# Moving five of the six transpose turns of the mixed features of batches 3 and 4 one slot later

## Chip, cores, metric

The kernel runs on one core of a Trainium2 chip. The metric is the device time of one execution in microseconds (us). All runs told of here are of the fast state (none is over 1.5% above the fastest of its kernel); TensorE's granted clock is 0.992 to 1.0 of full speed on average over an execution. That last per cent matters below.

## The reference, in short

```python
# 1. mLSTM cell over q, k, v and gates: (4 batches, 8 heads, 768 tokens, 40) -> x (4, 768, 320)
# 2. Fourier mix and MLP on x:
mixed = np.real(np.fft.fft(np.fft.fft(x, axis=1), axis=2))
u = x + mixed
un = (u - mean(u)) / np.sqrt(var(u) + 1e-06)          # over the 320 features
out = u + np.maximum(un @ w_ch1, 0.0) @ w_ch2         # 320 -> 1280 -> 320
```

## The kernel before

The four batches are pipelined. Work is put down in slots, and each engine's program is the list of its instructions sorted by slot and phase. While the second layer of the MLP of batch n-1 runs on TensorE (`po`, one block of 20 products in most slots), batch n's features are mixed in. For each of six token chunks, in the order c = 0, 5, 1, 4, 2, 3, this is

- an addition on VectorE of the mixed features `pu` (in PSUM) to x, and the statistics of the sum (lines 746 to 757 of the profile);
- a turn: centring on ScalarE (`uc`, L765), three transposes on TensorE (`put`, L772), a copy from PSUM on ScalarE (`uT`, L777).

Two chunks share one `pu`: 0 and 5, 1 and 4, 2 and 3. For batches 3 and 4 (b = 2 and 3 in the code) the PSUM banks are pinned:

```python
# cut from several places; NT = 6 chunks, TG = 3; DM = 320, HALF_D = 160, NC = 161
ORDER = (0, 5, 1, 4, 2, 3)
...
MIX = {"z": (2, 3), "zt": 2, "u": (3, 2, 2), "ut": (3, 3, 3, 3, 2, 3)}
# pu of chunks 0/5: bank 3; of 1/4 and of 2/3: bank 2.
# put in ORDER: bank 3, but bank 2 for c=2
...
def mix_add(b, c):
    k = mixes[b]
    k.u = xs[b]
    ops = (OP.subtract, OP.add) if c >= NT // 2 else (OP.add, OP.subtract)
    u, n = k.u[:, c, 0:DM], HALF_D - 1
    pu = k.pu[min(c, NT - 1 - c)]
    P, Q = pu[:, 0:NC], pu[:, NC:DM]
    if c == TG:
        own = pu[0:1, DM + 1:]
        if b == 0:
            nc.vector.tensor_copy(out=pu[0:1, 0:HALF_D], in_=own[:, 0:HALF_D])
            nc.vector.tensor_copy(out=pu[0:1, HALF_D:DM + 1], in_=backwards(own, HALF_D, NC))
        else:
            nc.vector.tensor_copy(out=P[0:1], in_=own)
            nc.vector.memset(Q[0:1], 0.0)
    if b == 0:
        nc.vector.tensor_tensor(out=u, in0=u, in1=pu[:, 0:DM] if c < TG else backwards(pu, DM, DM), op=OP.add)
    else:
        nc.vector.tensor_tensor(out=u[:, 0:NC], in0=u[:, 0:NC], in1=P, op=OP.add)
        nc.vector.tensor_tensor(out=u[:, NC:], in0=u[:, NC:], in1=backwards(P, n, n), op=OP.add)
        nc.vector.tensor_tensor(out=u[:, 1:HALF_D], in0=u[:, 1:HALF_D], in1=Q, op=ops[0])
        nc.vector.tensor_tensor(out=u[:, NC:], in0=u[:, NC:], in1=backwards(Q, n - 1, n), op=ops[1])
    stats = st_p.tile([L, 6], FP, name="stats", tag="stats")
    nc.vector.bn_stats(stats, u[:, 0:DM])
    nc.vector.bn_aggr(k.u[:, c, DM:], stats)

def mix_center(b, c):
    k = mixes[b]
    u = k.u[:, c]
    uc = k.uc[c] = st_p.tile([L, 2, L + 64], FP, name="uc", tag="uc")
    twice = bass.AP(tensor=u.tensor, offset=u.offset, ap=[list(u.ap[0]), [L, 2], [1, L + 64]])
    nc.scalar.activation(out=uc, in_=twice, func=AF.Identity, scale=-1.0, bias=u[:, DM:DM + 1])

def mix_turn(b, c):
    k = mixes[b]
    pt = k.pt[c] = bank("put", [L, 3, L], MIX["ut"][ORDER.index(c)] if b > 1 else None)
    for ch in range(3):
        nc.tensor.transpose(pt[:, ch, :], k.uc[c].rearrange("p two n -> p (two n)")[:, ch * L:(ch + 1) * L], ident)

def mix_turn_out(b, c):
    k = mixes[b]
    n = ORDER.index(c)
    nc.scalar.copy(out=uT_bufs[n // TG][:, :, n % TG, :], in_=k.pt[c])
```

The plan of additions (a), and of the three parts of a turn (t). The phases in a slot are EVAC = 0, FILL = 1, MAIN = 2, FILL_PE = 3; the `po` block and its two residuals (L949 on VectorE, x = x + rstd * po) are at MAIN, so an addition at MAIN + 0.5 stands behind both residuals of its slot.

```python
    for c, a, t in zip(ORDER, s_add, s_turn):
        at(a, FILL if b < 2 else MAIN + 0.5, mix_add, b, c)
        at(t, FILL + 0.1, mix_center, b, c)
        at(t, FILL_PE + (5 if b == 0 or c in ORDER[:4] else -0.1), mix_turn, b, c)
        if b > 0:
            at(t, FILL_PE + 6, mix_turn_out, b, c)
        elif t < s_mlp:
            at(t + 1, FILL + 0.2, mix_turn_out, b, c)
        else:
            at(t + 1, EVAC, mix_turn_out, b, c)
...
# in plan_batch, batches 2 to 4
        feat = [s_mix + c for c in ((3, 4, 6) if b == 1 else (3, 4, 7))]
        add = [s_mix + c for c in ((4, 4, 5, 6, 7, 7) if b == 1 else (4, 4, 5, 6, 8, 9))]
        turn = [s_mix + c for c in ((5, 6, 6) if b == 1 else (5, 6, 7))]
        late = [s_mix + c for c in ((7, 8, 8) if b == 1 else (8, 9, 10))]
```

The last slot of a batch's stage is s_mix + 11; then the next stage, the first MLP layer (`pm`), begins with sums of `uT` on VectorE (L885).

## Time and profile before

| | before |
|---|---|
| median time | 427.93 us (4 executions) |
| span of the profiled execution | 425.2 us |
| TensorE busy | 409.2 us, 96% |
| TensorE waiting for the last addition, ahead of `put` | 4.3 us in 2 waits |
| batch 3's stretch: first `pu` of batch 3 to first `pm` of batch 3 | 238.06 to 277.20: 39.14 us |
| batch 4's stretch: from there to the `pm` of batch 4 that waits for L885 | 277.20 to 360.50: 83.30 us |

The two stretches hold everything that the change touches; I measure by them below. How the wait of batch 3 is read is shown in the prediction. Its twin in batch 4, on TensorE's timeline of the kernel before (start, duration, what, idle time before it and what ended it):

```profile
349.02 1.52 PE L999 MATMUL po<-T,S 128*128 128x160 f32 x10
350.38 1.52 PE L999 MATMUL po<-w_sb,S 128*128 128x160 f32 x10
354.04 0.52 PE L772 MATMUL put<-ident,uc 128*128 128x128 f32 x3 [2.13 <-DVE x L754]
```

Groups of ten `po` products start 1.36 apart; the prediction reckons from this how late `put` came (step a).

### The profile page before, as it was taken

The page shows a single profiled execution, that of the slowest core. Times are in us where ns is not written, and L with a number is a line of the kernel's source. Part 1 is how long each engine was busy: PE and PEld are TensorE (multiplying, and loading weights), DVE is VectorE, ACT ScalarE, POOL GpSimd, SP SyncE. Part 2 cuts the span into 40 slices and gives each one's busy share as a digit, 9 for nine tenths or more (in the row PEclk, how much of TensorE's full clock was granted, in tenths as well). Part 3 has the DMA queues.
Part 4 walks back from the last instruction along what each step waited for, and adds up shares of the span by engine and source line. Part 5 has one row for each costly group of instructions (what it writes and reads, how often), then busy time and mean ns, then how long its engine had stood idle before and what let it go on. Part 6 is the DMA issues. An engine that isn't in the chain of part 4 may idle for free.

```text
span 425.2 us, 7994 instructions
## 1 busy us (share of the span) xinstructions
PE 409.2 (96%) x2966; PEld 302.7 (71%) x2966; DVE 288.4 (68%) x682; ACT 189.8 (45%) x493; POOL 113.1 (27%) x194
## 2 busy tenths in 40 slices
PE   8999999999999999999999999799999997999997
PEld 6877555566567777776459998776459996445996
DVE  7789895767986557878655768778554785334552
ACT  6986376586651233554563343454450122355000
POOL 5654201468332421250401431440300000020000
DMA  7889297657664244267000725200000000000010
GB/s 227 271 240 341 70 280 239 195 192 216 220 175 144 79 129 145 89 198 217 2 0 2 216 82 179 77 15 1 0 2 0 32 32 32 0 2 0 15 47 32
DMA packets 20549, 47.14 MB, mean 111 GB/s; under 512 B 2784, under 2 KB 9312, under 8 KB 20384
## 3 DMA queue, kind: packets, MB, share of 16 engines
q1 hardware_dynamic: 20512, 46.65, 35.5%
q8 instruction: 23, 0.38, 0.4%
q14 instruction: 14, 0.11, 0.1%
HBM read 42.52 MB, written 4.11 MB: 110 GB/s over the span
## 4 chain that ended last, share of the span: by engine, by line
PE 86%; DVE 9%; ACT 3%; issue 1%; POOL 0%; ACTq 0%; DVEq 0%
PE po L999 18%; PE pm L897 17%; PE po L943 8%; PE ps L465 6%; PE ph L486 5%; PE pm L837 5%; PE pm L902 5%; PE ph L479 4%; PE pu L729 4%; PE px L535 2%; PE put L772 2%; DVE S L985 2%; PE pz L698 2%; PE pm L841 1%; PE pc L496 1%
## 5 line engine op out<-in xcount | busy, mean ns | idle before, releaser
L949 DVE SCALAR_TENSOR_TENSOR x<-po,rstd,x 128x160 f32<-128x160 f32 (+1 forms) x69 | 27.1, 395 | 44.5 <-PE po L999 37.9
L906 DVE TENSOR_TENSOR h<-h,pm 128x384 f32<-128x384 f32 x60 | 30.5, 550 | 33.1 <-ACT h L919 24.7
L443 POOL TENSOR_SCALAR_AFFINE_SELECT W<-W 128x1024 f32<-128x1024 f32 x18 | 21.4, 1190 | 91.0 <-ACT W L421 70.6
L421 ACT ACTIVATE W<-W,colT 128x128 f32<-128x128 f32 x144 | 45.1, 395 | 0.0
L943 PE MATMUL po<-w_sb,h 128*128 128x320 f32 x120 | 34.4, 435 | 0.0
L471 DVE TENSOR_TENSOR W<-ps,W 128x512 f32<-128x512 f32 x48 | 30.7, 680 | 4.5 <-POOL W L443 4.3
L897 PE MATMUL pm<-uT,w_sb 128*128 128x384 f32 x90 | 32.8, 492 | 0.2 <-DVE uT L885 0.2
L777 ACT COPY uT<-put 128x384 f32<-128x384 f32 x24 | 11.3, 478 | 48.5 <-PE put L772 48.5
L837 PE MATMUL pm<-uT,w_sb 128*128 128x384 f32 x80 | 29.7, 500 | 0.7 <-DVE x L749 0.5
L943 PEld LDWEIGHTS po<-w_sb,h 128*128 128x128 f32 x120 | 22.2, 190 | 9.5 <-issue 0.8
L999 PE MATMUL po<-T,S 128*128 128x160 f32 x180 | 27.8, 301 | 0.5 <-DVE x L949 0.4
L465 PE MATMUL ps<-qk 40*128 40x128 f32 x384 | 27.8, 284 | 0.0
L792 POOL TENSOR_TENSOR t<-rstd 128x6 f32<-128x6 f32 x12 | 2.9, 244 | 91.9 <-DVE v L790 91.3
L999 PE MATMUL po<-w_sb,h 128*128 128x160 f32 x180 | 26.2, 301 | 1.1 <-DVE h L906 1.1
L999 PEld LDWEIGHTS po<-T,S 128*128 128x128 f32 x180 | 25.5, 190 | 2.2 <-DVE x L949 1.4
L999 PEld LDWEIGHTS po<-w_sb,h 128*128 128x128 f32 x180 | 24.9, 190 | 2.8 <-DVE h L906 2.4
L465 PEld LDWEIGHTS ps<-qk 40*128 40x128 f32 x384 | 23.4, 187 | 4.2 <-issue 0.7
L486 PE MATMUL ph<-W,kvt 128*41 128x128 f32 x384 | 25.8, 276 | 0.0
L431 POOL TENSOR_TENSOR qg<-qk,Gb 128x512 f32<-128x512 f32 x18 | 25.0, 1388 | 0.1
L479 PEld LDWEIGHTS ph<-qg,C 128*128 128x128 f32 x160 | 20.0, 191 | 6.2 <-issue 2.0
L897 PEld LDWEIGHTS pm<-uT,w_sb 128*128 128x128 f32 x90 | 16.2, 190 | 10.9 <-DVE h L906 1.5
L936 ACT ACTIVATE h<-h 128x384 f32<-128x384 f32 x45 | 23.0, 524 | 1.5 <-DVE h L906 1.5
(207 smaller groups left out, 852.8 us busy)
## 6 DMA issues: line engine op xcount, KB each, us to landing
W<-M_d SPq DMA_DIRECT2D x18, 512.0 KB
kvt<-in_kv SPq DMA_DIRECT2D x24, 324.0 KB
qk<-in_qkT SPq DMA_DIRECT2D x48, 160.0 KB
raw<-in_w SPq DMA_DIRECT2D x10, 640.0 KB
Gb<-G_d SPq DMA_DIRECT2D x36, 128.0 KB
so<-in_o SPq DMA_DIRECT2D x24, 160.0 KB
out<-x SPq DMA_DIRECT2D x24, 160.0 KB
ds_sb<-in_dft_s SPq DMA_DIRECT2D x1, 1155.0 KB
```

The lines of the kernel that those rows point to most:

```text
L421: nc.scalar.activation(out=k.W[:, h, :], in_=M, func=AF.Exp, scale=-1.0, bias=colT[:, c, 0, b * H + h:b * H + h + 1])
L431: nc.gpsimd.tensor_tensor(out=k.qg, in0=k.qk[:, 0], in1=k.Gb, op=OP.mult)
L465: nc.tensor.matmul(k.ps[hip][:, p, :], k.qk[r, 1, p, :], k.qk[r, 0, p, :], start=True, stop=True)
L471: nc.vector.tensor_tensor(out=Wv, in0=k.ps[hip], in1=Wv, op=OP.mult)
L479: nc.tensor.matmul(k.ph[:, p, :], k.C[:, p, :], k.qg[:, p, :], start=(p == 0), stop=False, skip_group_check=True)
L486: nc.tensor.matmul(k.ph[hip * 64:hip * 64 + D1, p, :], k.v1[:, 2 * p + hip, :], k.W[:, 2 * p + hip, :], start=(c == 0 and p == 0), stop=Tr ...
L837: nc.tensor.matmul(k.pm[i], w1_sb[:, ch, f0:f0 + L], u[2 * ch], start=(ch == 0), stop=False)
L897: nc.tensor.matmul(bank, w, u, start=start, stop=True, skip_group_check=True)
L906: nc.vector.tensor_tensor(out=h, in0=h, in1=bank, op=OP.add)
L943: nc.tensor.matmul(k.po, hidden(gr, f)[:, i * L:(i + 1) * L], w2_sb[:, f, :], start=(f == 0), stop=(f == NFF - 1))
L949: nc.vector.scalar_tensor_tensor(out=u, in0=po, scalar=k.rstd[:, c:c + 1], in1=u, op0=OP.mult, op1=OP.add)
L999: nc.tensor.matmul(po, a[:, f], w[:, f], start=start and f == 0, stop=f == half - 1, skip_group_check=True)
```

## The change

The intent is to take c=2's transposes away from the place where they wait for the last additions to leave bank 2. The first five turns of batches 3 and 4 go one slot later; the sixth stays, and shares its slot with the fifth.

```diff
-            turn = [s_mix + c for c in ((5, 6, 6) if b == 1 else (5, 6, 7))]
-            late = [s_mix + c for c in ((7, 8, 8) if b == 1 else (8, 9, 10))]
+            turn = [s_mix + c for c in ((5, 6, 6) if b == 1 else (6, 7, 8))]
+            late = [s_mix + c for c in ((7, 8, 8) if b == 1 else (9, 10, 10))]
```

## The prediction

> **What bounds the kernel now.** I read the page's busy shares and chain first, then the list of what TensorE waited for, then the timelines of TensorE, VectorE (DVE) and ScalarE (ACT) in the two stretches that the change touches. Times are us from the span's start.
>
> ```profile
> PE 409.2 (96%) x2966; PEld 302.7 (71%) x2966; DVE 288.4 (68%) x682; ACT 189.8 (45%) x493; POOL 113.1 (27%) x194
> PE 86%; DVE 9%; ACT 3%; issue 1%; POOL 0%; ACTq 0%; DVEq 0%
> PE put L772 <- DVE x L754: 4.3, 2, 2.1
> PE put L772 <- ACT uc L765: 1.3, 4, 0.4
> ```
>
> TensorE is busy 96% and carries 86% of the chain that ended last, so time returns only if TensorE stands still less. Its longest named wait is the third line: the turn's transposes (put, L772) waited twice, 2.1 us each, for the last of VectorE's additions to x (L754). The two waits are one in each of batches 3 and 4. Batch 3's, first TensorE, then VectorE, then ScalarE:
>
> ```profile
> 263.22 0.55 PE L772 MATMUL put<-ident,uc 128*128 128x128 f32 x3
> 263.61 1.52 PE L999 MATMUL po<-T,S 128*128 128x160 f32 x10
> 264.97 1.52 PE L999 MATMUL po<-w_sb,S 128*128 128x160 f32 x10
> 268.62 0.52 PE L772 MATMUL put<-ident,uc 128*128 128x128 f32 x3 [2.13 <-DVE x L754]
> 268.97 1.52 PE L999 MATMUL po<-T,S 128*128 128x160 f32 x10
> ```
> ```profile
> 266.53 0.38 DVE L949 SCALAR_TENSOR_TENSOR x<-po,rstd,x 128x160 f32<-128x160 f32 x1 [0.97 <-PE po L999]
> 266.83 0.31 DVE L746 COPY pu<-pu 1x161 f32<-1x161 f32 x1
> 267.23 0.19 DVE L747 MEMSET pu<- 1x159 f32 x1
> 268.16 0.31 DVE L754 TENSOR_TENSOR x<-x,pu 128x159 f32<-128x159 f32 x1
> 268.51 0.49 DVE L756 BATCH_NORM_STATS2 stats<-x 128x6 f32<-128x320 f32 x1
> 269.04 0.18 DVE L757 BATCH_NORM_AGGREGATE x<-stats 128x2 f32<-128x6 f32 x1
> ```
> ```profile
> 263.81 0.48 ACT L777 COPY uT<-put 128x384 f32<-128x384 f32 x1 [4.33 <-PE put L772]
> 264.18 1.28 ACT L421 ACTIVATE W<-W,colT 128x128 f32<-128x128 f32 x4
> 266.25 0.61 ACT L765 ACTIVATE uc<-x 128x384 f32<-128x384 f32 x1
> ```
>
> The reader is to see a closed loop. The stalled transposes are those of the fifth chunk (c=2); they write PSUM bank 2. The additions of the sixth chunk (c=3) still read that bank, because both chunks share one feature tile, pu. Those additions stand in VectorE's program behind the residual of the very po block that TensorE has just finished (266.53). So TensorE must finish po, then wait for the residual, the two fixes of pu's first row and four additions, before it may overwrite bank 2. Batch 4 has the same figure: po ends, residual at 351.94, last addition at 353.58, transposes at 354.04 after 2.13 us idle.
>
> **What the Trainium skill says.** "PSUM — Partial Sum Buffer", section "PSUM bank collisions raise a hardware error", asks that PSUM be guarded by semaphores by bank and quadrant, not by address. The trace agrees: put starts at 268.62, 0.15 us after the last read of the bank ended (268.16 + 0.31 = 268.47). The same page, "Engine vs sequencer instructions", says that the ScalarE and VectorE queues are strict FIFO; so here: the c=2 centring (uc, 266.25) came after the exponentials that stand ahead of it, though its data had been there since 263.57 (L757 at 263.39, 0.18 long). "Perfetto Trace Analysis", section "Matmuls", wants independent groups to rotate through banks so that evacuation overlaps the next group; bank 2, held by pu and wanted by put, is the place where this kernel doesn't. The page states no cost for such a wait; I take it from the trace.
>
> **The change part by part.** Nothing is added or removed: the engines run the same instructions. A turn is a centring (ACT, 0.61 us), three transposes (PE) and a copy out (ACT, 0.48 us). In batches 3 and 4 the turns of the chunks, in their order c = 0, 5, 1, 4, 2, 3, go one slot later, except the last, which stays; the last two then share a slot. A slot holds one po block of 20 products (10 in every fourth). The instruction orders of the two kernels confirm it: PE now has each put one po block later and, at the end, six put transposes in a row; ACT has the two centrings in a row and then the two copies; POOL and SP are unchanged, and VectorE differs only in buffer numbers.
>
> I count from start to start on TensorE, since its modelled ends overlap. A block of 20 po products takes 2.72 (263.61 to 264.97, twice), an unstalled put 0.33 behind po.
>
> (a) Removed: the c=2 wait. Without it put would start at 263.61 + 2.72 = 266.33; it started at 268.62. That is 2.29 us. Batch 4: 349.02 + 2.72 = 351.74 against 354.04, 2.30 us. Moved behind the next po block, these transposes need bank 2 at about 0.33 (the put now in that place) + 2.72 = 3.05 after 266.33, while VectorE lets it go at 2.29. The wait is covered whole. Sum: -4.6 us.
>
> (b) Removed in batch 3: the wait of the second turn (c=5) for its centring. The po block before it starts at 249.42, so put was due at 252.14 and came at 252.73: 0.59 us. ACT had there a copy, four exponentials, h, so, then uc. In the new order the exponentials run earlier, straight after the four before them, and the place of this put is taken by c=0's, whose centring has only h and so ahead of it. Sum: -0.6 us.
>
> (c) Added in batch 3: the same ACT sequence (copy, four exponentials, h, so, uc) stands before the put that now takes c=2's old place, that of c=4. Today that uc ends at 266.25 + 0.61 = 266.86 and with some 0.05 for the signal put could start at 266.91, against 266.33: 0.58 us that the longer bank wait hides today and that now shows. Sum: +0.6 us, which cancels (b).
>
> (d) Added: the last turn (c=3) comes earlier relative to the additions it needs, since c=2's put no longer stalls in front. Counted from the due time of the put before (266.33, or 351.74): the statistics end at 2.89 (269.04 + 0.18, batch 3) or 2.89 (batch 4, 354.45 + 0.18). ACT starts 0.10 later, works 0.62, and 0.05 for the signal makes 3.66. TensorE reaches this put at 0.33 + 2.72 + 0.33 = 3.38 in batch 4: it waits 0.28 us. In batch 3 it comes there 0.6 later because of (c): no wait. Sum: +0.3 us.
>
> (e) What follows. In batch 4 the next block's entry is gated by VectorE: the residual of the last po block (359.00), then the sums of uT (L885), then pm at 360.50. That tail starts from the end of po, 1.36 us behind the last put; the two copies need about 0.5 after that put, so the tail moves with it. In batch 3 VectorE's mask product (L471, 1.26 us) and residual follow the c=3 additions; they end near 4.3 on the same count, TensorE needs them at about 4.7 (put, put, px): no new wait. Sum: 0.
>
> Total: -4.6 - 0.6 + 0.6 + 0.3 = -4.3 us, so 428.0 becomes 423.7, about 1.0% faster.
>
> **The rivals.**
> First, the wait is only handed on: six transposes at the end of the stage wait for the last centring. For it: ACT is in order and the c=3 statistics arrive late on the count above. Against it: (d) gives 0.3 us, not 2. If centring were also held up by other ACT work, each batch would lose up to 1 us more: 425.5.
> Second, the gain is given back where the next stage begins, because VectorE or the attention work interleaved there (masks on POOL, W loads) doesn't come earlier. For it: VectorE is the second engine on the chain (9%), and around 274 to 280 it works with little pause. Against: TensorE waits there for nothing, 277.2 to 314.3 is one unbroken stretch of PE, and VectorE's part follows PE's own px and po. If one batch's gain were lost: 425.9.
> Third, the ACT wait (c) doesn't appear and (b) does vanish: 423.1; the better case. For it: some exponentials now run earlier. Against: those ahead of c=4's centring are the same ones in the same place.
>
> **Range and chances.** 423.7 predicted; between the third rival and about two thirds of the loss of the first, 422.7 to 425.2 should hold 8 times in 10. Over 2% faster would need 8.6 us, and all TensorE waits of these two stages together are little over half of that: 0.02. Over 2% slower would need a stall in the new order longer than any now in the trace: 0.01. Within 2%: 0.97.
>
> **What would show it right or wrong.** Right: the list of waits has no put behind L754 any more; a put behind uc of roughly 0.4 us idle (0.6 start to start) at c=4 of batch 3 and a shorter one at the last put of batch 4; none at c=5 of batch 3; pm of batch 3 starts about 2.3 us sooner (277.20 before) and pm of batch 4 about 4.3 us sooner (360.50 before). Wrong: put waiting over 1 us for uc; pm, po or ph in the next stage waiting for VectorE or ACT where they don't today; or a pm of batch 4 that is early while the end isn't.

## The result

The changed kernel takes 423.22 us (median of 4, 422.23 to 423.68) against 427.93 us (427.69 to 428.09). The ratio is 0.9887, 95% interval 0.9867 to 0.9907: 1.1% faster. Ratios are the mean time of one kernel's fast runs over that of the other's of the same rounds, so not quite the ratio of the medians.

The page of the profile after, its busy shares, and the list of what TensorE waited for:

```profile
span 420.5 us, 7995 instructions
PE 408.1 (97%) x2966; PEld 301.8 (72%) x2966; DVE 287.5 (68%) x682; ACT 189.6 (45%) x493; POOL 112.0 (27%) x194
```
```profile
PE put L772 <- ACT uc L765: 1.2, 4, 0.4
PE po L999 <- DVE x L949: 0.6, 2, 0.4
```

The wait for L754 is gone from the list. The waits of `put` for centrings are no longer in sum than before (1.2 against 1.3). A wait of `po` for the residual L949, of which the list before had one of 0.4 us, now counts two and 0.6 us.

Batch 3, TensorE, changed kernel:

```profile
263.28 1.52 PE L999 MATMUL po<-w_sb,S 128*128 128x160 f32 x10
265.23 0.55 PE L772 MATMUL put<-ident,uc 128*128 128x128 f32 x3 [0.42 <-ACT uc L765]
266.97 1.52 PE L999 MATMUL po<-w_sb,s_last 128*128 128x160 f32 x10
268.33 0.82 PE L772 MATMUL put<-ident,uc 128*128 128x128 f32 x6
274.17 1.56 PE L897 MATMUL pm<-uT,w_sb 128*128 128x384 f32 x4
```

The second line is c=4's `put`, which now stands where c=2's stood: due at 263.28 + 1.36 = 264.64, started at 265.23. The fourth is the pair of c=2 and c=3: six transposes in one run, 1.36 after the `po` line ahead of it, so without a wait. Batch 4, first the kernel before, where the window asked for ends within the third line, then the changed kernel:

```profile
337.49 1.52 PE L999 MATMUL po<-w_sb,S 128*128 128x160 f32 x10
338.85 0.49 PE L772 MATMUL put<-ident,uc 128*128 128x128 f32 x3
339.27 0.95 PE L999 MATMUL po<-T,S 128*128 128x160 f32 x5
```

```profile
334.46 1.52 PE L999 MATMUL po<-w_sb,S 128*128 128x160 f32 x10
336.24 1.62 PE L999 MATMUL po<-T,S 128*128 128x160 f32 x10 [0.25 <-DVE x L949]
351.80 1.16 PE L772 MATMUL put<-ident,uc 128*128 128x128 f32 x6
355.85 0.91 PE L897 MATMUL pm<-uT,w_sb 128*128 128x384 f32 x2 [0.24 <-DVE uT L885]
```

The reader is to see two things. In the second line of the changed kernel a `po` block starts 336.24 - 334.46 = 1.78 after the one before, 0.42 late, waiting for a residual. Before, c=0's `put` stood between these two, and they were as far apart (339.27 - 337.49 = 1.78): taking the `put` away from there gained nothing. And the six transposes take 1.16 here, 0.82 in batch 3: there is a gap inside. The chain that ended last, in order of time, shows what lies in it (start, duration, what; pieces of "issue" between them left out):

```profile
351.46 0.19 DVE x L757
351.73 0.62 ACT uc L765
352.40 0.55 PE put L772 x3
```

c=3's transposes start at 352.40, though c=2's three need only 0.33 from 351.80; they wait 0.27 us for the statistics and the centring.

Batch 3's stretch is now 237.30 to 274.17 = 36.87 us (-2.27), batch 4's 274.17 to 355.85 = 81.68 us (-1.62): together -3.89. The rest of the 4.7 us by which the two traces' spans differ lies ahead of the first `pu` (238.06 against 237.30), where both kernels run the same instructions.

### The profile page after: what moved, and what is told of

The parts are those of the page before. It is cut to its first block, busy times and chain, and to the rows that moved or that the text cites. A ratio compares the mean times of both kernels' runs of the same rounds, so it can differ in the third digit from the quotient of the medians.

```text
span 420.5 us, 7995 instructions
## 1 busy us (share of the span) xinstructions
PE 408.1 (97%) x2966; PEld 301.8 (72%) x2966; DVE 287.5 (68%) x682; ACT 189.6 (45%) x493; POOL 112.0 (27%) x194
## 4 chain that ended last, share of the span: by engine, by line
PE 77%; DVE 12%; DMA 7%; ACT 2%; issue 1%; POOL 0%; SPq 0%; DVEq 0%; ACTq 0%
PE pm L897 17%; PE po L999 16%; PE po L943 8%; PE ps L465 5%; PE pm L902 5%; PE ph L486 5%; PE ph L479 4%; DMA kvt<-in_kv 3%; PE pm L837 3%; PE pu L729 3%; DVE S L985 2%; PE px L535 2%; DMA qk<-in_qkT 2%; PE pz L698 2%; PE put L772 1%; DVE x L949 1%
## 5 line engine op out<-in xcount | busy, mean ns | idle before, releaser
L949 DVE SCALAR_TENSOR_TENSOR x<-po,rstd,x 128x160 f32<-128x160 f32 (+1 forms) x69 | 27.0, 394 | 41.6 <-PE po L999 35.0
L524 ACT COPY h<-ph 41x512 f32<-41x512 f32 (+1 forms) x16 | 9.3, 582 | 35.5 <-PE ph L486 35.4
```

What stands on the lines that cost most here:

```text
L949: nc.vector.scalar_tensor_tensor(out=u, in0=po, scalar=k.rstd[:, c:c + 1], in1=u, op0=OP.mult, op1=OP.add)
```

## The experiments

Twelve runs, each timed in 5 rounds. The stretches are what I read first, because three traces of the changed kernel give them as 36.87, 36.88, 36.87 and 81.68, 81.68, 81.67, while the time ahead of them differs from execution to execution: the first `pu` of batch 3 starts anywhere from 237.30 to 240.26 in the traces of this study. The fast runs of before on the three chips that were used have medians 428.78, 427.74 and 428.45.

| run | batch 3's stretch | batch 4's | sum against before | median us | ratio, 95% interval |
|---|---|---|---|---|---|
| before | 39.14 | 83.30 | | | |
| whole_change | 36.88 | 81.68 | -3.88 | 423.63 | 0.9881, 0.9850 to 0.9912 |
| only_c2_later | 37.53 | 81.60 | -3.31 | 424.98 | 0.9908, 0.9877 to 0.9938 |
| all_but_c2 | 40.21 | 83.64 | +1.41 | 428.63 | 0.9996, 0.9973 to 1.0020 |
| other_bank | 37.53 | 81.59 | -3.32 | 424.39 | 0.9894, 0.9863 to 0.9926 |
| filled_stall | 39.14 | 83.28 | -0.02 | 428.16 | 0.9999, 0.9975 to 1.0023 |
| early_centre | 36.60 | 81.62 | -4.22 | 424.12 | 0.9902, 0.9869 to 0.9934 |
| late_add | 36.86 | 82.38 | -3.20 | 425.05 | 0.9920, 0.9889 to 0.9950 |
| all_waits | 36.22 | 82.04 | -4.18 | 422.96 | 0.9876, 0.9846 to 0.9906 |
| change_again | 36.87 | 81.67 | -3.90 | 424.63 | 0.9905, 0.9881 to 0.9928 |
| first_two_kept | 36.87 | 81.36 | -4.21 | 424.38 | 0.9901, 0.9878 to 0.9925 |
| early_fix | 36.87 | 81.34 | -4.23 | 423.81 | 0.9902, 0.9877 to 0.9927 |
| best | 36.23 | 81.02 | -5.19 | 422.64 | 0.9867, 0.9841 to 0.9892 |

### The change again, and its parts: is it the fifth turn alone?

No edit: the changed kernel.

> The changed kernel once more, for a narrower interval. Between the two traces the stretches of batches 3 and 4 account for 3.9 us (2.28 in batch 3, 1.62 in batch 4), and 0.75 us more lies ahead of them, where both kernels run the same instructions. If that 0.75 is only the wobble of one execution, the time is 424.0 us against 427.9 (ratio 0.991). If the change also pays elsewhere, it is 423.2 (0.989) again.

The stretches repeat to 0.01 us. The time ratio again says more (about 5 us) than the stretches do. What makes up the rest is taken up with the clock below.

Only the fifth turn moved:

```diff
-            late = [s_mix + c for c in (... else (8, 9, 10))]
+            late = [s_mix + c for c in (... else (8, 10, 10))]
```

> Before, with only the fifth turn (c=2) of batches 3 and 4 one slot later, all other turns in their old places. Theory (the bank wait of c=2 is the whole cause): both waits of 2.3 us go, and the last turn, now 0.33 us nearer to its additions, waits about 0.6 us in each batch: gain 4.6 - 1.2 = 3.4 us, 424.5 us. The wait of c=5 for its centring in batch 3 stays. Rival (the other turns, with the exponentials that come earlier on ScalarE, carry the gain): under 1 us, above 427 us.

As the theory has it: -3.31 us by the stretches against -3.4, and both waits for L754 are gone. The price is the expected one: c=3's `put` waits 0.45 us idle for its centring, in both batches.

All turns but the fifth moved:

```diff
-            turn = ... (5, 6, 7)      late = ... (8, 9, 10)
+            turn = ... (6, 7, 8)      late = ... (9, 9, 10)
```

> The change without its fifth turn: c=0, 5, 1, 4 one slot later, c=2 in its old place. Theory: the two waits of 2.1 us idle for the last addition stay in the list; batch 3 loses the 0.6 us wait of c=5, batch 4 gets 0.3 us for the residual that stands behind two chunks of additions: 427.6 us, the same as before within half a us. Rival (the other turns carry it): 424 to 425 us.

The two waits stay, 2.13 us idle each, and the time is that of before (428.63 against 428.78): the other turns carry next to none of the gain (0.3 us of the stretches, if the dip told of below is taken off). Batch 4's +0.34 is as expected; batch 3's +1.07 against the expected -0.6 is not. TensorE's timeline there, and then the busy time of each engine and the granted clock (PEclk) in two windows:

```profile
267.78 0.99 PE L772 MATMUL put<-ident,uc 128*128 128x128 f32 x6 [2.13 <-DVE x L754]
268.56 2.88 PE L999 MATMUL po<-T,S 128*128 128x160 f32 x10
271.23 1.78 PE L999 MATMUL po<-w_sb,s_last 128*128 128x160 f32 x10
```
```profile
core 0: us, PE busy (x) PEld busy (x) DVE busy (x) ACT busy (x) POOL busy (x), PEclk, DMA share, GB/s
240.00:268.00 28.00, 25.87 (x249) 24.09 (x248) 21.99 (x66) 8.23 (x22) 9.30 (x12) 1.00 0.42 134
268.00:273.00 5.00, 5.00 (x28) 5.00 (x27) 1.90 (x5) 1.37 (x3) 0.73 (x1) 0.66 0.23 56
```

Ten `po` products take 271.23 - 268.56 = 2.67 us instead of 1.36, the next ten 1.62 (to the `put` at 272.85). Nothing is waited for; the granted clock is 0.66 in these 5 us, right after the standstill. That costs 1.3 + 0.3 us there and 0.1 in the six transposes; without it the stretch would be 1.7 shorter, -0.6, as expected. Asked for each us from 268 to 273, the same view gives a granted clock of 0.67, 0.50, 0.50, 0.62 and 1.00. That is half of full speed for some 3.4 us, and 0.33 + 0.50 + 0.50 + 0.38 = 1.7 us of full speed lost. The stall of batch 4 in the same trace, as long, was followed by no dip (1.00 from 355 to 362).

### The bank, or the place?

```diff
-    MIX = {..., "ut": (3, 3, 3, 3, 2, 3)}
+    MIX = {..., "ut": (3, 3, 3, 3, 3, 3)}
```

> Before, with all turns in their old slots, and only the PSUM bank of c=2's transposes changed from 2 to 3. Theory (it is the bank, not the slot): no put waits for the last addition; in batch 3 put of c=2 waits for its centring instead, 0.6 us start to start, in batch 4 for nothing: gain 2.3 - 0.6 + 2.3 = 4.0 us, 423.9 us. Rival (it is the place behind the additions on VectorE or the statistics that hold it): no gain, 427.9 us.

One digit in place of the moved slots takes both waits away: the bank is what tied TensorE to the last additions. In the rest the expectation was 0.7 us too good: in batch 4, c=3's `put` waits for its centring here too (0.42 us idle), as where only the fifth turn was moved. I had reckoned that wait for the moved slots and forgotten that it comes whenever c=2's `put` no longer stalls ahead of it.

### The granted clock

The idle products take a bank number for this (that line of the edit is left out here).

```diff
+            if b > 1 and c == TG - 1:                       # c = 2
+                at(t, FILL_PE - 0.15, idle_products, 4, 3)  # 4 products of zeros into bank 3
```

> Before, with four idle products (about 1.7 us of TensorE work on zeros into bank 3, read by nobody) put into each of the two stalls ahead of c=2's transposes. In the runs so far, 9 of 19 executions of before and 9 of 14 of the variant that keeps the stalls have a mean granted clock of 0.992 to 0.996, and none of the 22 of the three variants without them (0.999 at least). Theory (a 2.1 us standstill of TensorE now and then costs a stretch of halved clock): with the stalls filled no execution is below 0.999, the stages are as long as before (39.1 and 83.3 us) and the time is that of before's executions at clock 0.999 or more, 427.8 us, 0.7 to 1 us below the median of before. Rival (the dips come from elsewhere, and the variants without them are luck): about half of the executions still show 0.996, same time as before.

The products fill 267.24 to 269.13 of the stall in batch 3, the idle time shrinks from 2.13 to 0.40 us, and the stretches keep their length. One of 14 executions is below 0.999 (0.995), against 7 of 19 of before on the same chip. So the standstill has much to do with the dips, but not everything: one dip is left here, and one of the six executions of early_centre, which has no such stall, shows 0.996. Alone, 1 of 14 against 7 of 19 could be chance (about one in ten by an exact test); with the counts below it is unlikely to be. The time didn't follow. The ratio is 0.9999, with an interval of a good us to either side, so the 0.7 us or so that I expected is neither shown nor ruled out. The 13 executions without a dip average 427.9 us here and the 12 of before on this chip 427.3, though the stretches are equal; why is not known.

Counted over all runs that record it: below 0.999 are 20 of 49 executions of before and 9 of 14 of all_but_c2, which have the stalls; 1 of 14 with the stalls filled; 1 of 64 in the eleven runs of kernels without the stalls. The 20 of before average 429.4 us, its other 29 average 427.6.

### The terms of the sum

ScalarE's order (step c):

```diff
-            at(t, FILL + 0.1, mix_center, b, c)
+            at(t, FILL - 0.6 if b == 2 else FILL + 0.1, mix_center, b, c)
```

> The changed kernel, with batch 3's centrings moved ahead of the exponentials and copies of their slots on ScalarE. Theory (step c: the new wait of c=4's put is ScalarE's queue order): the 0.42 us wait of put for uc in batch 3 goes, and 0.3 to 0.6 us of batch 3's stretch (36.87 us) with it, the lower figure where c=3's put then waits for its own centring; 423.1 to 423.4 against 423.7 of the changed kernel. Rival (the exponentials now come late, and the mask product or the attention products wait): no gain, or a new wait of ph, pm or px.

TensorE's timeline of batch 3 in this run:

```profile
267.34 0.49 PE L772 MATMUL put<-ident,uc 128*128 128x128 f32 x3
270.39 1.16 PE L772 MATMUL put<-ident,uc 128*128 128x128 f32 x6
```

c=4's `put` no longer waits; the six now take 1.16 as in batch 4, since c=3's comes early enough to wait for its own centring. The stretch is 0.27 us shorter, the lower figure of the expectation. The wait of c=4 was ScalarE's order.

The residual in batch 4:

```diff
-            add = ... else (4, 4, 5, 6, 8, 9)
+            add = ... (4, 5, 5, 6, 8, 9) if b == 3 else (4, 4, 5, 6, 8, 9)
```

> The changed kernel, with the second chunk's addition (c=5) of batch 4 one slot later, behind the next residuals on VectorE. Theory (the term that the prediction missed: po of batch 4 waits 0.25 us idle, 0.42 start to start, for a residual that stands behind two chunks of additions, which c=0's put used to cover): that wait goes, the stretch of batch 4 falls from 81.68 to 81.35 us. Rival: the later addition makes pu or put of c=5 or c=0 wait instead: 81.7 us or more.

A miss: the wait moved one slot on and grew. `po` now waits 1.00 us there for a residual that stands behind c=5's and c=1's additions:

```profile
342.54 1.63 PE L999 MATMUL po<-T,h 128*128 128x160 f32 x10 [1.00 <-DVE x L949]
```

Both together, and pu's first-row fixes a slot earlier:

```diff
 # mix_add
-        if c == TG:
+        if c == TG and b < 2:
...
+        if b > 1 and c == TG - 1:          # behind c=2's addition and statistics
+            nc.vector.tensor_copy(out=P[0:1], in_=pu[0:1, DM + 1:])
+            nc.vector.memset(Q[0:1], 0.0)
```

> Both of these together, and pu's two first-row fixes done right after c=2's additions, a slot earlier, so that c=3's additions end about 0.6 us sooner and its put waits no more. Theory: batch 3's stretch 36.87 - 0.58 = 36.3 us, batch 4's 81.68 - 0.33 - 0.28 = 81.1 us, 1.2 us below the changed kernel: 422.5 us. Rival: VectorE has too little room in those slots and the gain is under 0.4 us.

Batch 3 is as expected (36.22). Batch 4 keeps late_add's loss, less 0.34 by the early fixes. So the late addition was dropped, and the two other remedies were tried alone, beside the change itself:

> The changed kernel beside the next three on one chip. Batch 3's stretch 36.87 us, batch 4's 81.68 us, as in both traces of it so far; no execution below clock 0.999; about 4 us below before, 5 with the slow clock of some of before's executions.

This came out as before: the stretches to 0.01 us, lowest clock 0.999, 3.8 us between the medians.

```diff
 # first_two_kept
-            turn = [s_mix + c for c in (... else (6, 7, 8))]
+            turn = [s_mix + c for c in (... else (5, 6, 8) if b == 3 else (6, 7, 8))]
```

> The changed kernel with the first two turns of batch 4 (c=0, 5) back in their old slots, so that c=0's put again stands ahead of the po block that waits for a residual. Theory (the missed term is that uncovered residual): the wait of po for the residual goes and batch 4's stretch is 81.68 - 0.33 = 81.35 us; as c=5's put no longer stands ahead of the last features there, they may then wait up to 0.3 us for bank 2 (the additions end 0.04 ahead of them today), and the stretch stays at 81.6. Batch 3 unchanged.

81.36: the residual's wait is gone, and the features do not wait for bank 2.

The early fixes alone:

> The changed kernel with pu's first-row fixes right after c=2's additions. Theory (step d: c=3's put in batch 4 waits because the additions and statistics end late): the last put's wait for uc in batch 4 goes, 81.68 - 0.34 = 81.34 us; batch 3 stays at 36.87, as its last put doesn't wait. Rival (it waits for ScalarE, not for the statistics): 81.68 as before.

81.34, the figure of the expectation; the wait of the last `put` in batch 4 is gone (its six transposes take 0.82). It waited for the statistics, and so for the additions.

### A version that beats both

Early centring in batch 3, early fixes, and batch 4's first two turns in their old slots:

> The changed kernel with the early centring in batch 3, the early fixes, and batch 4's first two turns in their old slots. From the parts: batch 3's stretch 36.2 us, batch 4's 81.0 us (81.3 if the last features wait for bank 2), 1.0 to 1.3 us below the changed kernel on this chip.

The stretches are 36.23 and 81.02, 1.30 us less than the change's in sum, and no `put` of these batches waits. Median 422.64 us against 424.63 for the change on the same chip; the ratio to before is 0.9867. The intervals of the two ratios overlap, so the stretches are the firmer evidence that it beats the change.

## Why the prediction was right

The predicted 423.7 and the measured 423.22 (and 423.63, 424.63 in the repeats) agree. The mechanism was right; that the number fits to 0.5 us is partly luck, as the end of this section shows. By the prediction's own marks, `pm` came 3.03 us sooner in batch 3 and 4.65 in batch 4 (2.3 and 4.3 predicted), but 0.76 of each lies ahead of the stretches, so I go by those. Step by step:

- (a), the two waits for bank 2, -4.6: right. Both are gone; moving the fifth turn alone, or changing its bank alone, each takes them away, and moving all turns but the fifth leaves them.
- (b) and (c), one ScalarE wait removed and one added in batch 3: right. c=5's `put` doesn't wait; c=4's comes 0.59 late against the reckoned 0.58. The early centring shows that its cause is ScalarE's order.
- (d), c=3's `put` in batch 4, +0.28: right, 0.27. The early fixes take away 0.34.
- (e), "Sum: 0": wrong by 0.33 us. It looked at the tails of the stages and not at what the removed `put` had covered at the front. In batch 4, `po` of the third slot needs a residual that VectorE runs behind two chunks of additions. Before, c=0's `put` stood there, and `po` started 0.42 after it (338.85 to 339.27) where 0.33 is its own length; 0.09 was waiting. With the `put` gone, all 0.42 is waiting. first_two_kept, which puts it back, gains 0.31.

So the sum of the stretches is -3.89 rather than -4.3; 0.33 of the difference is (e), the other 0.08 is spread over steps of a few hundredths. Yet the first medians differ by 4.7, which the prediction's terms do not explain. What can account for it, though this is argued and not shown, is the clock: 20 of 49 executions of before ran with a dip, and these average 1.8 us more than the others (429.4 against 427.6), which is the size of the one dip seen in a trace (1.7). Spread over all executions that is 1.8 * 20 / 49 = 0.7 us, which the change saves as well, because its executions, 16 in three runs, showed no dip. 3.9 + 0.7 = 4.6 us. But the four executions of before in the first comparison have no clock on record, and its traced one ran at 1.000; between the two traces it is the time ahead of the stretches that differs (by 0.76). In the repeats, the means differ by 4.8 us on one chip and by 4.0 on another. So the agreement of the medians rests on a missed cost of 0.4 us and some 0.8 us of gain or chance that the prediction did not have. That the stalls bring dips is shown by the counts, and by one trace; that filling the stalls gives 0.7 us back was not shown.

Of the rivals, the first (the wait is only handed on) is true to the 0.27 us of (d). The third (no wait at c=4) did not happen: 0.59. The second (given back at the next stage) did not happen: from the `pm` at the end of batch 4's stretch to the end the traces of both kernels take 64.7 us. The bounds of the range, 422.7 and 425.2, are some 0.3 to 0.4 us wider than its own words give (423.1 for the third rival, 424.9 for two thirds of the first's loss); every median of the change lies within them. What makes the time ahead of batch 3's stretch differ by up to 3 us from execution to execution was not looked into, and stays open.

## What to carry to other kernels

When TensorE waits to overwrite a PSUM bank, first ask whether another bank is free at that moment: here that one digit was worth 3.3 us, nearly as much as moving five turns (3.9). When an instruction is moved off a stall, look at both places: what it used to cover where it stood (0.33 us here), and which wait was hidden beneath the one removed (0.27 us and 0.6 us here). And when executions differ by more than the term in question, compare the length of the stretch that the change touches in the traces: here it repeats to 0.02 us, where the whole time does not to 2, unless a dip of the clock falls into it (1.7 us in all_but_c2).

## What the Trainium skill lacked or had wrong

- "TensorE: Matmul & The Clock Gate", section "Why this matters for your kernels", advises against TensorE idle gaps above some 3 us. Here a gap of 2.13 us was followed by some 3.4 us at half clock (0.66 on average over 5 us), and 29 of 63 executions of the two kernels with such gaps were below 0.999, against 1 of 14 with the gaps filled to 0.40 us. Gaps well under 3 us can matter, though not each time: an equal one in the same trace was followed by no dip.
- The same page, section "Part 4: PE-mode transpose", gives the duration of a single transpose (bf16: some 390 ns in isolation, some 275 ns in a kernel). The trace agrees with the second (273 ns at the median, fp32 in the profile), but what a plan needs is the spacing: three in a row move the next product by only 0.33 us.
- "Perfetto Trace Analysis", section "Matmuls", advises rotating through PSUM banks and names no price for not doing so. In this case it was 2.3 us for each of two waits.
